# Four heads' decayed values on VectorE, w_in's conversion begun later, and decay tables made on the chip

## The chip, the cores and the metric

The kernel runs on one core of a Trainium2 chip. The metric is device time in microseconds (us), lower is better. A core has five instruction streams: TensorE (PE in the rows; PEld is its weight load), VectorE (DVE), ScalarE (ACT), GpSimd (POOL) and SyncE (SP), and 16 DMA engines that move data between device memory and the core's SBUF. Each stream is executed in its own order; what holds an instruction back is a semaphore that another stream or a DMA raises.

## The reference, cut to what matters

Three parts follow each other. The change touches only the first one and a preparation that runs beside it.

1. Decayed linear attention over 4 sequences of 768 tokens, 8 heads of 64: for each token, `state = gamma_h * state + k v^T` and `y = 0.125 * q state`, with `gamma_h = 1 - 2^(-5-h)`.
2. A capacity-limited mixture of experts: logits `x @ w_gate`, a greedy assignment of 3072 tokens to 8 experts of 384 places, and for each expert `relu(x w1) w2`.
3. A dense layer on the result: `softplus(x w_in) w_out`. All arithmetic has to keep fp32 quality, so the kernel splits weights and activations into a high and a low part of TensorE's reduced fp32 type and multiplies three times.

## The kernel before, in words

**Attention (class Attn).** The 24 chunks are 4 sequences of 6 chunks of 128 tokens. For one chunk TensorE computes: `qk` (L125, tile pA: k^T q of all heads, 16 products), which VectorE multiplies by the causal decay mask out of PSUM (L126, tile at); `y` (L142 within the chunk, and L138 from the state with decayed queries qs; tile pY), copied by ScalarE (L145, yT); `kv` (L155, tile pS: the state's update from decayed values vh), copied by ScalarE (L157, sb); and `xo` (L164, tile pX: yT times a matrix rx that transposes it and appends the 8 gate columns), copied by ScalarE (L168, xs) and stored by SP (L178). VectorE sums the four partial gate columns of pX (L173, `gate`) into L. The tiles pA, pX, pY and pS exist once each, so TensorE's `qk` of a chunk waits until `at` of the chunk before is read out, and its `xo` until both xs and the gate's sum of the chunk before are done.

Two decays come from the host. `qs` is q times a table (L106, GpSimd); the table has one 256 KB slice for each chunk of a sequence but the first, and SP loads that slice just before the chunk's q and k (L98). `vh` is v times one factor for each token and head (L108 to L115): eight ScalarE instructions of 128x64, one a head, for every chunk but a sequence's last.

The turn of the loop for chunk j (`emit`, L187) records in this order: load q,k of chunk j+3; store chunk j-2; `qk` of j+1; a side step; `xo` of j-1; `y` of j; a side step; the gate's sum of j-1; `kv` of j; load k,v of j+3; `qs` of j+2; `vh` of j+1; at every sixth chunk a block of 12 short VectorE instructions (`logits`, L383 to L399) that ranks the last six chunks' gate logits; a side step. There is no scheduler: each engine runs what was recorded for it in the order of the text. The DMAs of SP and ScalarE take eight completion semaphores in turn, so a DMA is also not issued before the one eight places ahead of it has landed.

**Conversion of w_in (class Conv), in the side steps.** w_in arrives as 64-bit numbers, 16 pieces of 512 KB (raw, five buffers, L230). A piece takes two ScalarE passes (L241, L243), one on GpSimd (L242), then VectorE (L256, L258), GpSimd (L259), ScalarE (L269, the high part wih) and VectorE (L264, the low part wil). `cv.ahead()` (L927) records the loads of the first four pieces before the loop; the steps begin with the turn of chunk 1 and are spread over the turns until the last.

After the attention (about 128 us) come the routing of the first expert's tokens, and then the eight experts with their dense layer (up to the end of the span), which the change does not touch.

Of the kernel before, what the change touches and what calls it, by code (L numbers as in the profile page):

```python
# [9 lines left out]
FT = mybir.dt.float32  # L10
# [5 lines left out]
AF = mybir.ActivationFunctionType  # L16
OP = mybir.AluOpType
# [3 lines left out]
def shape_tables(H, S):  # L21


    g = 1.0 - 2.0 ** (-5.0 - np.arange(H, dtype=np.float64))
    i = np.arange(128)
    t = i[:, None] + 128 * np.arange(S // 128)
    gk = g ** (-t[:, :, None].astype(np.float64))
    m = np.where(i[:, None] <= i, 0.125 * g[:, None, None] ** (i - i[:, None]).clip(0), 0.0)
    m = m.reshape(H // 2, 2, 128, 128).transpose(2, 1, 0, 3).reshape(128, -1)
    tab = np.concatenate([np.eye(128), m, gk.reshape(128, -1)], axis=1)  # L30
    gq = 0.125 * g[:, None] ** np.arange(S, dtype=np.float64)
    gq = np.repeat(gq.reshape(H // 2, 2, 1, S // 128, 128), 64, axis=2)
    gq = gq.transpose(1, 2, 3, 0, 4).reshape(128, -1)
    return tab.astype(np.float32), gq.astype(np.float32)


# [17 lines left out]
class Attn:  # L54
# [4 lines left out]
    def __init__(self, tc, ctx, ps, qk, kv, w_gate, tab, gqt, ident, L, xd, B, H, S):  # L59
        nc = self.nc = tc.nc  # L60
        self.ps = ps
        self.qk_in, self.kv_in, self.gq_in, self.L, self.xd, self.ident = qk, kv, gqt, L, xd, ident
        self.B, self.H, self.S = B, H, S
        self.NC = S // 128
        self.NCH = B * self.NC
        self.HP = HP = H // 2
        c = ctx.enter_context(tc.tile_pool(name="acst", bufs=1, side="right"))
        self.ld = ctx.enter_context(tc.tile_pool(name="ald", bufs=3, side="right"))
        self.wk = ctx.enter_context(tc.tile_pool(name="awk", bufs=2, side="right"))
        self.t = {}  # L70
        self.gq = c.tile([128, self.NC - 1, 512], FT, name="gqt")
        n = tab.shape[1] - 128
        ct = c.tile([128, n], FT, name="ctab")
        self.load(0, "qk")
        nc.scalar.dma_start(ct, tab[:, 128:])
        self.load(0, "kv")
        nc.scalar.dma_start(ident, tab[:, 0:128])
        self.cm = ct[:, 0:1024].rearrange("p (s a t) -> p s a t", s=2, a=HP)
        self.gk = ct[:, 1024:n].rearrange("p (c h) -> p c h", h=self.H)
        self.load(1)  # L80
        self.load(2)
        self.sb = []
        for i in range(2):
            self.sb.append(c.tile([128, HP, 64], FT, name=f"sb{i}"))
        self.rx = c.tile([128, HP, 136], FT, name="rx")
        nc.scalar.dma_start(self.rx[:, :, 128:136], w_gate.rearrange("(a p) e -> p a e", p=128))
        self.pS = self.ps.tile([128, HP, 128], FT, name="pS")
# [6 lines left out]
    def load(self, j, which=("qk", "kv")):  # L94
        for n in (which,) if isinstance(which, str) else which:
            t = self.t[n, j] = self.ld.tile([128, 2, 512], FT, name=n + "_t", bufs=4)
            if n == "qk" and 0 < j < self.NC:
                self.nc.sync.dma_start(self.gq[:, j - 1], self.gq_in[:, j * 512:(j + 1) * 512])  # L98
            self.nc.sync.dma_start(t, (self.qk_in if n == "qk" else self.kv_in)[j])

    def scale(self, j):

        c, nc = j % self.NC, self.nc
        if c:
            qs = self.t["qs", j] = self.wk.tile([128, self.HP, 128], FT, name="qs", bufs=2)
            nc.gpsimd.tensor_mul(qs.rearrange("p a t -> p (a t)"), self.t["qk", j][:, 0], self.gq[:, c - 1])  # L106

    def scale_v(self, j):  # L108

        c, nc = j % self.NC, self.nc  # L110
        if c < self.NC - 1:
            vh = self.t["vh", j] = self.wk.tile([128, self.H, 64], FT, name="vh", bufs=2)
            for h in range(self.H):
                nc.scalar.activation(vh[:, h], self.t["kv", j][:, 1, h * 64:h * 64 + 64], AF.Copy,
                                     scale=self.gk[:, c, h:h + 1])  # L115

    def qk(self, j):
        nc = self.nc
# [62 lines left out]
    def emit(self, side, logits):  # L181
        n = self.NCH
        self.qk(0)
        self.scale_v(0)
        self.scale(1)
        self.late_constants()
        for j in range(n):  # L187
            if j + 3 < n:
                self.load(j + 3, "qk")
            self.store(j - 2)  # L190
            if j + 1 < n:
                self.qk(j + 1)
            side(j, 0)
            if j:
                self.xo(j - 1)
            self.y(j)
            side(j, 1)
            if j:
                self.gate(j - 1)
            self.kv(j)  # L200
            if j + 3 < n:
                self.load(j + 3, "kv")
            if j + 2 < n:
                self.scale(j + 2)
            if j + 1 < n:
                self.scale_v(j + 1)
            if j:
                logits(j - 1)
            side(j, 2)
        self.store(n - 2)  # L210
        self.xo(n - 1)
        self.gate(n - 1)
        self.store(n - 1)
        logits(n - 1)
# [6 lines left out]
class Conv:  # L221
# [6 lines left out]
    def load(self, p):  # L228
        raw = self.raw[p] = self.st.tile([128, self.W, 2], I32, name="raw", bufs=self.bufs)
        self.nc.sync.dma_start(raw.rearrange("p n b -> p (n b)"), self.plan[p][0])  # L230

    def ahead(self, p=0):
        while self.loaded < min(p + self.bufs - 1, len(self.plan)):
            self.load(self.loaded)
            self.loaded += 1
# [659 lines left out]
def model(ctx, tc, qk, kv, w_gate, w1, w2, w_in, w_out, tab, gqt, out, B, H, S):  # L895
    nc = tc.nc
# [17 lines left out]
    cv = Conv(tc, c1, 512, cuts, 5, 2, (5, 4))  # L914
# [2 lines left out]
    a = Attn(tc, c2, aps, qk, kv, w_gate, tab, gqt, ident, L, xd, B, H, S)  # L917

    def side(j, part):
        if j:  # L920
            cv.step((3 * j - 2 + part) * 50 // 69)

    def logits(j):
        if j % 6 == 5:
            R.first_part(j - 5, j + 1)

    cv.ahead()  # L927
    a.emit(side, logits)
    cv.step(1000)
    c2.close()  # L930
# [41 lines left out]
```

## Time and profile before

| | |
|---|---|
| time, median of 3 runs | 1037.16 us (1035.96 to 1038.77) |
| the profiled execution | 1039.39 us, of which the span of the rows is 1037.6 us |
| TensorE busy | 994.5 us, 96% of the span |
| VectorE / ScalarE / GpSimd busy | 61% / 56% / 18% of the span |
| mean granted clock of TensorE | 0.987 |

Times in rows are microseconds from the span's start. A row of the timeline gives start, duration, engine, line, operation, output <- inputs, shapes, the count, and in brackets how long the engine had been idle before it and what ended that; instructions of one kind that follow each other are drawn together. In the rows by window a number after the window is its length, then busy time and instruction count of each engine, then the granted clock as a share of full speed, the mean busy share of the DMA engines and their GB/s.

### The profile page before, as it was taken

The numbers are of one execution on the slowest core, as the hardware profiler recorded it, in microseconds if no ns is written. First come the engines' busy times: TensorE is split into PE (matmuls) and PEld (weight loads), VectorE is DVE, ScalarE is ACT, GpSimd is POOL, SyncE is SP. The second block draws the span as 40 slices with busy tenths as digits, with TensorE's granted clock in tenths as the row PEclk, the third lists the DMA queues.
The fourth block names the chain that finished last, engine by engine and source line by source line (L and its number), as shares of the span: only waits on it lengthen the run. The fifth ranks groups of instructions, "written<-read, shape, count | busy, mean of one in ns | idle before, by whom it ended". The sixth has DMA issues, their size and how long they took to land.

```text
span 1037.6 us, 19094 instructions
## 1 busy us (share of the span) xinstructions
PE 994.5 (96%) x7266; PEld 901.9 (87%) x7266; DVE 636.3 (61%) x1649; ACT 585.0 (56%) x1245; POOL 186.1 (18%) x204
## 2 busy tenths in 40 slices
PE   5999878999999999999999999999999999999997
PEld 4888757978899889988998889888989899999996
DVE  3686687888766666766575567555665644454432
ACT  4897723676645563566446644665356546654664
POOL 4685422556210101010101010100010020001001
PEclk9998999999999999999999999999999999999999
DMA  9998434423141104110321023101410160014000
GB/s 358 401 405 306 146 96 137 128 82 112 54 142 32 31 21 124 50 31 11 117 67 32 11 92 92 31 1 52 122 32 1 52 192 1 1 41 123 1 1 31
DMA packets 41179, 97.55 MB, mean 94 GB/s; under 512 B 5376, under 2 KB 5504, under 8 KB 41088
## 3 DMA queue, kind: packets, MB, share of 16 engines
q1 hardware_dynamic: 36432, 83.12, 24.1%
q0 software_dynamic: 3840, 12.59, 3.7%
q8 instruction: 57, 0.93, 0.4%
q10 hardware_dynamic: 816, 0.63, 0.2%
q14 instruction: 34, 0.28, 0.1%
HBM read 83.73 MB, written 12.58 MB: 93 GB/s over the span
## 4 chain that ended last, share of the span: by engine, by line
PE 72%; issue 12%; POOL 5%; DVE 5%; DMA 2%; ACT 2%; another core or an unknown queue 0%; SPq 0%; ACTq 0%; POOLq 0%
PE h L659 11%; PE h L662 11%; PE h L660 10%; PE acc L757 7%; PE acc L762 7%; PE acc L758 7%; PE acc L651 3%; PE acc L653 3%; PE acc L652 3%; PE pX L164 2%; POOL wol L259 2%; PE pA L125 2%; POOL cA L242 2%; PE pY L142 2%; PE rt L406 2%
## 5 line engine op out<-in xcount | busy, mean ns | idle before, releaser
L723 DVE SCALAR_TENSOR_TENSOR gf<-h,sp 128x384 f32<-128x384 f32 x128 | 71.2, 556 | 185.2 <-ACT sp L721 185.0
L659 PE MATMUL h<-x2h,wih 128*128 128x384 f32 x512 | 176.5, 345 | 2.0 <-DVE xl L647 2.0
L660 PE MATMUL h<-x2h,wil 128*128 128x384 f32 x512 | 173.3, 338 | 0.0
L757 PE MATMUL acc<-whi,gh 128*128 128x512 f32 x384 | 153.2, 399 | 0.0
L758 PE MATMUL acc<-wlo,gh 128*128 128x512 f32 x384 | 151.2, 394 | 0.0
L719 ACT ACTIVATE sp<-h 128x384 f32<-128x384 f32 x128 | 62.6, 489 | 137.5 <-PE h L662 127.2
L643 ACT ACTIVATE h1h<-h 128x384 fp32r<-128x384 f32 x64 | 31.5, 492 | 148.8 <-PE h L662 105.5
L770 POOL DMA_INDIRECT out_dram<-rows,ix x24 | 25.3, 1053 | 501.4 <-ACT rows L768 498.0
L662 PE MATMUL h<-x2l,wih 128*128 128x384 f32 x512 | 112.8, 340 | 0.8 <-DVE x2l L647 0.6
L762 PE MATMUL acc<-whi,gl 128*128 128x512 f32 x384 | 111.2, 396 | 0.8 <-DVE gl L737 0.8
L659 PEld LDWEIGHTS h<-x2h,wih 128*128 128x128 f32 x512 | 96.6, 189 | 5.8 <-DVE xl L647 2.2
L660 PEld LDWEIGHTS h<-x2h,wil 128*128 128x128 f32 x512 | 96.6, 189 | 3.4
L662 PEld LDWEIGHTS h<-x2l,wih 128*128 128x128 f32 x512 | 92.1, 189 | 2.9 <-DVE x2l L647 2.9
L637 DVE TENSOR_TENSOR wlo<-wraw,whi 128x512 fp32r<-128x512 f32 x128 | 86.3, 689 | 6.1 <-ACT whi L636 6.1
L659 PE MATMUL h<-xh,whi 128*128 128x384 f32 x256 | 89.0, 348 | 0.7 <-ACT xh L646 0.7
L637 DVE TENSOR_TENSOR wlo<-wol,whi 128x512 fp32r<-128x512 f32 x128 | 89.0, 698 | 0.9 <-ACT whi L636 0.9
L651 PE MATMUL acc<-h1h,whi 128*128 128x384 f32 x256 | 88.4, 345 | 0.0
L762 PEld LDWEIGHTS acc<-whi,gl 128*128 128x128 f32 x384 | 72.0, 188 | 18.6 <-DVE gl L737 1.4
L660 PE MATMUL h<-xh,wlo 128*128 128x384 f32 x256 | 86.8, 339 | 0.0
L636 ACT ACTIVATE whi<-wraw 128x512 fp32r<-128x512 f32 x128 | 76.6, 624 | 17.1 <-DMA wraw<-in_moe_w_dram 14.2
L653 PE MATMUL acc<-h1l,whi 128*128 128x384 f32 x256 | 86.1, 336 | 0.0
L652 PE MATMUL acc<-h1h,wlo 128*128 128x384 f32 x256 | 86.1, 336 | 0.0
(201 smaller groups left out, 1932.1 us busy)
## 6 DMA issues: line engine op xcount, KB each, us to landing
wraw<-in_moe_w_dram SPq DMA_DIRECT2D x128, 256.0 KB, 2.7
qk_t<-in_qk_dram SPq DMA_DIRECT2D x24, 512.0 KB, 8.8
kv_t<-in_kv_dram SPq DMA_DIRECT2D x24, 512.0 KB, 6.4
raw<-in_moe_w_in_dram SPq DMA_DIRECT2D x16, 512.0 KB, 7.0
raw<-in_moe_w_out_dram SPq DMA_DIRECT2D x32, 256.0 KB, 2.8
xd<-xs SPq DMA_DIRECT2D x24, 256.0 KB, 4.7
gqt<-in_gqt_dram SPq DMA_DIRECT2D x5, 256.0 KB
ctab<-in_tab_dram ACTq DMA_DIRECT2D x1, 536.0 KB
```

What stands on the lines that cost most here:

```text
L636: nc.scalar.activation(hi, raw, AF.Copy)
L637: nc.vector.tensor_tensor(lo, raw, hi.bitcast(FT), op=OP.subtract)
L651: nc.tensor.matmul(ps, wh, ah, start=start, stop=False)
L652: nc.tensor.matmul(ps, wl, ah, start=False, stop=False)
L653: nc.tensor.matmul(ps, wh, al, start=False, stop=stop)
L659: mm(ps, wh(d), ah[:, d], start=d == 0, stop=False)
L660: mm(ps, wl(d), ah[:, d], start=False, stop=False)
L662: mm(ps, wh(d), al[:, d], start=False, stop=d == 3)
L723: nc.vector.scalar_tensor_tensor(g, ps, 0.0, a, op0=OP.max, op1=OP.add)
L757: nc.tensor.matmul(ps, gh[:, s], wh, start=f == 0, stop=False)
L758: nc.tensor.matmul(ps, gh[:, s], wl, start=False, stop=False)
L762: nc.tensor.matmul(ps, gl[:, s], wh, start=False, stop=f == 15)
```

## The change

Four edits, all in the attention.

- `vh`: ScalarE keeps heads 0 to 3 (four instructions of 128x64); heads 4 to 7 become one VectorE product of 128x256 (v times the factors, broadcast over 64 columns), recorded behind them.
- The decay table of q: the host sends one chunk's table and the 20 step factors (`gqb`, 128x532, one DMA on ScalarE's queue, 272 KB); in the first sequence `scale(j)` makes each chunk's slice by four VectorE instructions of 128x128. SP's five slice loads are gone.
- w_in: no load is recorded before the loop. `begin` records one load in each side step from chunk 2 on until four are out; the conversion steps start at chunk 4 and are spread over the turns 4 to 23.
- The gate's sum of chunk j-1 is recorded behind `vh` and the turn's last side step, just before `logits`.

```diff
--- before.py
+++ after.py
@@ -28,9 +28,11 @@
     m = np.where(i[:, None] <= i, 0.125 * g[:, None, None] ** (i - i[:, None]).clip(0), 0.0)
     m = m.reshape(H // 2, 2, 128, 128).transpose(2, 1, 0, 3).reshape(128, -1)
     tab = np.concatenate([np.eye(128), m, gk.reshape(128, -1)], axis=1)
-    gq = 0.125 * g[:, None] ** np.arange(S, dtype=np.float64)
-    gq = np.repeat(gq.reshape(H // 2, 2, 1, S // 128, 128), 64, axis=2)
-    gq = gq.transpose(1, 2, 3, 0, 4).reshape(128, -1)
+    gq = np.repeat((0.125 * g[:, None] ** i).reshape(H // 2, 2, 1, 128), 64, axis=2)
+    gq = gq.transpose(1, 2, 0, 3).reshape(128, -1)
+    gs = g[:, None] ** (128.0 * np.arange(1, S // 128))
+    gs = np.repeat(gs.reshape(H // 2, 2, 1, -1), 64, axis=2).transpose(1, 2, 3, 0).reshape(128, -1)
+    gq = np.concatenate([gs, gq], axis=1)
     return tab.astype(np.float32), gq.astype(np.float32)
 
 
@@ -71,8 +73,10 @@
         self.gq = c.tile([128, self.NC - 1, 512], FT, name="gqt")
         n = tab.shape[1] - 128
         ct = c.tile([128, n], FT, name="ctab")
+        self.gb = c.tile([128, gqt.shape[1]], FT, name="gqb")
         self.load(0, "qk")
         nc.scalar.dma_start(ct, tab[:, 128:])
+        nc.scalar.dma_start(self.gb, gqt)
         self.load(0, "kv")
         nc.scalar.dma_start(ident, tab[:, 0:128])
         self.cm = ct[:, 0:1024].rearrange("p (s a t) -> p s a t", s=2, a=HP)
@@ -94,13 +98,17 @@
     def load(self, j, which=("qk", "kv")):
         for n in (which,) if isinstance(which, str) else which:
             t = self.t[n, j] = self.ld.tile([128, 2, 512], FT, name=n + "_t", bufs=4)
-            if n == "qk" and 0 < j < self.NC:
-                self.nc.sync.dma_start(self.gq[:, j - 1], self.gq_in[:, j * 512:(j + 1) * 512])
             self.nc.sync.dma_start(t, (self.qk_in if n == "qk" else self.kv_in)[j])
 
     def scale(self, j):
 
         c, nc = j % self.NC, self.nc
+        if c and j == c:
+            n = (self.NC - 1) * self.HP
+            for hp in range(self.HP):
+                s = slice(hp * 128, hp * 128 + 128)
+                nc.vector.tensor_scalar(self.gq[:, c - 1, s], self.gb[:, n:][:, s],
+                                        self.gb[:, (c - 1) * self.HP + hp:(c - 1) * self.HP + hp + 1], None, op0=OP.mult)
         if c:
             qs = self.t["qs", j] = self.wk.tile([128, self.HP, 128], FT, name="qs", bufs=2)
             nc.gpsimd.tensor_mul(qs.rearrange("p a t -> p (a t)"), self.t["qk", j][:, 0], self.gq[:, c - 1])
@@ -110,9 +118,10 @@
         c, nc = j % self.NC, self.nc
         if c < self.NC - 1:
             vh = self.t["vh", j] = self.wk.tile([128, self.H, 64], FT, name="vh", bufs=2)
-            for h in range(self.H):
-                nc.scalar.activation(vh[:, h], self.t["kv", j][:, 1, h * 64:h * 64 + 64], AF.Copy,
-                                     scale=self.gk[:, c, h:h + 1])
+            v, n = self.t["kv", j][:, 1].rearrange("p (h d) -> p h d", d=64), self.H // 2
+            for h in range(n):
+                nc.scalar.activation(vh[:, h], v[:, h], AF.Copy, scale=self.gk[:, c, h:h + 1])
+            nc.vector.tensor_tensor(vh[:, n:], v[:, n:], self.gk[:, c, n:, None].to_broadcast([128, n, 64]), op=OP.mult)
 
     def qk(self, j):
         nc = self.nc
@@ -195,8 +204,6 @@
                 self.xo(j - 1)
             self.y(j)
             side(j, 1)
-            if j:
-                self.gate(j - 1)
             self.kv(j)
             if j + 3 < n:
                 self.load(j + 3, "kv")
@@ -204,9 +211,10 @@
                 self.scale(j + 2)
             if j + 1 < n:
                 self.scale_v(j + 1)
+            side(j, 2)
             if j:
+                self.gate(j - 1)
                 logits(j - 1)
-            side(j, 2)
         self.store(n - 2)
         self.xo(n - 1)
         self.gate(n - 1)
@@ -228,6 +236,11 @@
     def load(self, p):
         raw = self.raw[p] = self.st.tile([128, self.W, 2], I32, name="raw", bufs=self.bufs)
         self.nc.sync.dma_start(raw.rearrange("p n b -> p (n b)"), self.plan[p][0])
+
+    def begin(self):
+        if self.loaded < min(self.bufs - 1, len(self.plan)):
+            self.load(self.loaded)
+            self.loaded += 1
 
     def ahead(self, p=0):
         while self.loaded < min(p + self.bufs - 1, len(self.plan)):
@@ -917,14 +930,16 @@
     a = Attn(tc, c2, aps, qk, kv, w_gate, tab, gqt, ident, L, xd, B, H, S)
 
     def side(j, part):
-        if j:
-            cv.step((3 * j - 2 + part) * 50 // 69)
+        n = 3 * j + part
+        if n >= 6:
+            cv.begin()
+        if n >= 12:
+            cv.step((n - 11) * 50 // 60)
 
     def logits(j):
         if j % 6 == 5:
             R.first_part(j - 5, j + 1)
 
-    cv.ahead()
     a.emit(side, logits)
     cv.step(1000)
     c2.close()
```

SP's stream, at the loads of chunks 1 to 3 of the first sequence (qk_t is q and k of a chunk, kv_t its k and v, raw a piece of w_in, gqt a slice of the decay table). Before:

```order
L99 DMA kv_t_161<-in_kv_dram 128x1024
L98 DMA gqt_150<-in_gqt_dram 128x512 [waits DMAHW0_49]
L99 DMA qk_t_163<-in_qk_dram 128x1024 [waits DMAHW1_49]
L99 DMA kv_t_166<-in_kv_dram 128x1024 [waits DMAHW2_49]
L230 DMA raw_173<-in_moe2_w_in_dram 128x1024 [waits DMAHW3_49]
L230 DMA raw_175<-in_moe2_w_in_dram 128x1024 [waits DMAHW4_49]
L230 DMA raw_177<-in_moe2_w_in_dram 128x1024 [waits DMAHW5_49]
L230 DMA raw_179<-in_moe2_w_in_dram 128x1024 [waits DMAHW6_49]
L98 DMA gqt_150<-in_gqt_dram 128x512 [waits DMAHW7_49]
L99 DMA qk_t_207<-in_qk_dram 128x1024 [waits DMAHW0_49]
```

The same place now, from the load of k and v of chunk 1 on:

```order
L101 DMA kv_t_162<-in_kv_dram 128x1024
L101 DMA qk_t_164<-in_qk_dram 128x1024 [waits DMAHW0_49]
L101 DMA kv_t_166<-in_kv_dram 128x1024 [waits DMAHW1_49]
L101 DMA qk_t_200<-in_qk_dram 128x1024 [waits DMAHW2_49]
L101 DMA kv_t_233<-in_kv_dram 128x1024 [waits DMAHW3_49]
L101 DMA qk_t_247<-in_qk_dram 128x1024 [waits DMAHW4_49,PE_49]
L101 DMA kv_t_295<-in_kv_dram 128x1024 [waits DVE_49,DMAHW5_49,PE_49,Activation_49]
L101 DMA qk_t_310<-in_qk_dram 128x1024 [waits DMAHW6_49,Pool_49]
L187 DMA xd_63<-xs_265 128x512 [waits DMAHW7_49,Activation_49]
L238 DMA raw_324<-in_moe2_w_in_dram 128x1024 [waits DMAHW0_49]
```

The q and k of chunk 3 (qk_t_207 before, qk_t_200 now) stood behind four pieces of w_in and two table slices; now it stands where the first piece stood, and waits only for the semaphore that k and v of chunk 0 raise (DMAHW2).

VectorE's stream, in the turn of chunk 7, right behind the first `logits` block (whose last row is the first one shown). Before:

```order
L258 TENSOR_SCALAR cA_496<-cA_496 128x512
L126 TENSOR_TENSOR at_687<-pA_688,ctab_151 128x1024
L264 TENSOR_TENSOR wil_67<-cA_407,wih_66 128x4x128
L173 TENSOR_REDUCE L_64<-pX_698 128x8
L256 SCALAR_TENSOR_TENSOR cB_587<-raw_379,cB_587 128x512
L126 TENSOR_TENSOR at_755<-pA_756,ctab_151 128x1024
```

And now:

```order
L412 TENSOR_TENSOR G_140<-kx_139,thr0_85 128x276
L135 TENSOR_TENSOR at_659<-pA_660,ctab_151 128x1024
L277 TENSOR_TENSOR wil_67<-cA_491,wih_66 128x4x128
L269 SCALAR_TENSOR_TENSOR cB_565<-raw_394,cB_565 128x512
L124 TENSOR_TENSOR vh_714<-kv_t_569,ctab_151 128x256
L271 TENSOR_SCALAR cA_564<-cA_564 128x512
L182 TENSOR_REDUCE L_64<-pX_671 128x8
L135 TENSOR_TENSOR at_731<-pA_732,ctab_151 128x1024
```

The gate's sum (L173, now L182) has moved from the second place behind `at` to the fifth, just ahead of the next `at`, and the product of four heads' values (L124) and one more conversion step stand in front of it.

## Rows read from the trace of the kernel before

**Rows 1.** Three stretches of the attention by window (window, length, busy times, clock, DMA).

```profile
0.00:22.60 22.60, 10.97 (x136) 9.85 (x137) 7.39 (x29) 10.56 (x30) 7.34 (x20) 0.97 0.95 350
22.60:29.40 6.80, 6.77 (x72) 5.93 (x72) 2.35 (x4) 3.09 (x9) 5.58 (x6) 0.60 1.04 408
29.40:76.00 46.60, 45.71 (x732) 40.26 (x728) 34.05 (x63) 43.78 (x128) 33.57 (x24) 1.00 1.03 404
```

**Rows 2.** The chain that ended last, in the first 30 us (start, length, what).

```profile
1.69 10.43 DMA rx<-in_moe_w_gate_dram
...
13.46 9.04 DMA qk_t<-in_qk_dram
```

**Rows 3.** TensorE's timeline, chunks 2 to 4 and one undisturbed turn.

```profile
18.50 0.64 PE L155 MATMUL pS<-vh,kv_t 128*64 128x64 f32 x16
22.63 2.08 PE L125 MATMUL pA<-qk_t 64*128 64x128 f32 x16 [3.50 <-DMA qk_t<-in_qk_dram]
...
29.41 1.16 PE L125 MATMUL pA<-qk_t 64*128 64x128 f32 x16
...
55.64 1.16 PE L125 MATMUL pA<-qk_t 64*128 64x128 f32 x16
...
59.94 1.16 PE L125 MATMUL pA<-qk_t 64*128 64x128 f32 x16
```

**Rows 4.** SyncE's timeline: the first pieces of w_in.

```profile
8.39 4.55 SPq L230 DMA_DIRECT2D raw<-in_moe_w_in_dram  x4
```

**Rows 5.** DMA issues (KB each, median us to landing), from the page.

```profile
qk_t<-in_qk_dram SPq DMA_DIRECT2D x24, 512.0 KB, 8.8
...
raw<-in_moe_w_in_dram SPq DMA_DIRECT2D x16, 512.0 KB, 7.0
...
gqt<-in_gqt_dram SPq DMA_DIRECT2D x5, 256.0 KB
```

**Rows 6.** TensorE's timeline where it waited for the mask product `at`.

```profile
51.33 1.16 PE L125 MATMUL pA<-qk_t 64*128 64x128 f32 x16 [0.68 <-DVE at L126]
...
79.75 2.08 PE L125 MATMUL pA<-qk_t 64*128 64x128 f32 x16 [3.59 <-DVE at L126]
...
86.97 1.16 PE L125 MATMUL pA<-qk_t 64*128 64x128 f32 x16
...
109.60 1.16 PE L125 MATMUL pA<-qk_t 64*128 64x128 f32 x16 [1.53 <-DVE at L126]
```

**Rows 7.** The logits block on VectorE: held up by GpSimd, and alone (128.75 on).

```profile
75.09 2.50 POOL L106 TENSOR_TENSOR qs<-qk_t,gqt 128x512 f32<-128x512 f32 x2
75.18 1.20 DVE L394 SCALAR_TENSOR_TENSOR kf<-sg,unas 128x6 f32<-128x6 int32 x1
...
128.75 0.20 DVE L383 TENSOR_REDUCE m<-L 128x6 f32<-128x48 f32 x1
...
130.51 0.30 DVE L399 TENSOR_TENSOR G<-kx,thr 128x276 bf16<-128x276 f16 x1
```

**Rows 8.** The same VectorE product beside two kinds of GpSimd work.

```profile
55.01 1.27 POOL L259 TENSOR_TENSOR cA<-cA,cB 128x512 int32<-128x512 int32 x1 [0.36 <-DVE cA L258]
55.07 1.76 DVE L264 TENSOR_TENSOR wil<-cA,wih 128x512 fp32r<-128x512 f32 x1
...
82.03 1.49 POOL L242 TENSOR_SCALAR cA<-cA 128x512 f32<-128x512 f32 x1
83.02 0.68 DVE L264 TENSOR_TENSOR wil<-cA,wih 128x512 fp32r<-128x512 f32 x1
```

**Rows 9.** One chunk's decayed values on ScalarE, and a gate's sum that waited.

```profile
15.19 2.00 ACT L114 ACTIVATE vh<-kv_t,ctab 128x64 f32<-128x64 f32 x8
...
104.29 0.19 DVE L173 TENSOR_REDUCE L<-pX 128x8 f32<-128x32 f32 x1 [1.51 <-ACT xs L168]
```

**Rows 10.** VectorE's mask product by form, 29.4 to 76 us (count, busy, mean ns).

```profile
L126 DVE TENSOR_TENSOR at<-pA,ctab 128x1024 f32<-128x1024 f32 x10 | 12.2, 1221 | 6.4 <-PE pA L125 6.3
```

**Rows 11.** VectorE's timeline: the shift step of the conversion.

```profile
36.06 0.42 DVE L258 TENSOR_SCALAR cA<-cA 128x512 int32<-128x512 int32 x1
```

## The prediction

> **What bounds the kernel now.** I read the windows first, then the chain of waits, then TensorE's timeline. The change only touches the attention, the first 128 us; what follows is handed the same data and starts when the attention ends, so what it saves or costs there is taken one for one. In the windows [rows 1] the reader is to see two things. From 29.4 to 76 us TensorE is busy 45.71 of 46.60 us at the full clock, with the DMA engines full as well (share 1.03, 404 GB/s) and ScalarE nearly so (43.78 us). Ahead of that, in the first 22.6 us, TensorE is busy for less than half of the time while the DMA engines are already at 0.95, and in the next 6.8 us its granted clock is 0.60.
>
> The chain of waits says why [rows 2]: a small transfer (the gate's columns into rx) lands at 12.1 us and releases SP, which only then gets to issue q and k of chunk 3, at 13.46; those land 9.04 us later. In between SP had been issuing four pieces of w_in [rows 4]. TensorE's timeline shows the price [rows 3]: it ended chunk 1's state update at 18.50 + 0.64 = 19.14, stood idle for 3.50 us, and began chunk 3's products at 22.63 at the lower of its two clock levels (1.2 GHz: 16 products take 2.08 us, against 1.16 us at 2.4 GHz). The turn that begins there took 29.41 - 22.63 = 6.78 us; an undisturbed one takes 59.94 - 55.64 = 4.30.
>
> Later the bound is TensorE itself, but for three places where its next products waited for `at` on VectorE: 0.68, 3.59 and 1.53 us [rows 6], each right after a logits block. After the second one the clock was again at the lower level, and the turn took 86.97 - 79.75 = 7.22 us, 2.92 more than 4.30. The three cost 0.68 + 3.59 + 2.92 + 1.53 = 8.7 us.
>
> **The change part by part.**
>
> *Loads.* The four pieces of w_in (2.1 MB) and two table slices no longer stand ahead of chunk 3's q and k, which are now issued where the first piece was, at about 8.4 us [rows 4]. At 9.04 us to landing [rows 2], near the median of 8.8 [rows 5], they are there at 17.4 us, before TensorE asks at 19.14. The wait of 3.50 us goes, and with no idle stretch I expect the clock to stay up, so the 6.78 us turn becomes 4.30: 2.48 more. What is late next there is TensorE's own chain. Together -6.0 us. Bounds: if the landing slipped as much as 2 us more, about 1.7 + 0.3 us of it would be absorbed first, so 0 to -6.5.
>
> The five slices (1.28 MB) are replaced by one transfer of 0.27 MB on ScalarE's queue; it moves beside k and v of chunk 0 and q of chunk 1 as the first slice did. In the first turns I take 0, between -0.5 and +0.5 by its share at 0.35 MB a us [rows 1].
>
> *The same loads later.* The pieces return from chunk 2 on, four in two turns, and then 12 in the turns of chunks 4 to 17. A turn then moves 1.05 MB of q, k and v, 0.26 MB of stores and about 0.45 MB of w_in, 1.76 MB, or 4.36 us at 404 GB/s: the DMA engines, full at a turn of 4.30 before, want slightly more than a turn. I count what must have arrived when chunk 12 starts: 26 transfers of 0.52 MB, about 10 pieces, 8 stores and 0.9 MB of tables, 21.8 MB, so about 56 us from a start at 2 us. TensorE is ready for it at 23.4 + 8 x 4.2 = 57 us. That is 1 us of lead, where a transfer shares the engines with some that were issued after it. I charge +1.0 us; bounds 0 (the stops at the logits give lead) and +2.7: before, the 7.2 MB issued up to chunk 3's q and k would have been there at 2 + 7.2 / 0.404 = 19.8 us, and landed at 22.5 [rows 2], so a transfer wants up to 2.7 us of lead, and chunk 12 could lack it all.
>
> *Decayed values.* ScalarE gives up four of eight instructions, half of 2.00 us [rows 9], in 20 of 24 chunks. From 29.4 to 76 us it was busy 43.78 / 46.60 x 4.30 = 4.04 us a turn; it falls to about 3.5, with the denser conversion counted. That by itself does not move TensorE, but ScalarE's late xs had held the gate's sum, and behind it a logits block, by 1.51 us [rows 9]; that wait goes.
>
> The new VectorE product has 256 elements a partition from two SBUF inputs. No such row exists. Below it stands 0.30 us for 276 elements of 16 bits [rows 7], above it 0.68 us for 512 fp32 elements, alone, and 1.76 us when GpSimd is in the way [rows 8]. I take 0.4, near the shorter row. VectorE was busy 34.05 / 46.60 x 4.30 = 3.14 us a turn [rows 1]; with 0.33 for the product (five chunks of six) and 0.2 for the denser conversion it is at 3.7 of 4.30, with waits for GpSimd in it as they were. So it stays beside TensorE in an ordinary turn, with 0.6 us to spare: if that is gone, each turn costs the difference.
>
> *What stands against it.* A product that starts beside GpSimd's two-input addition took 1.76 us instead of 0.68: it ended 0.55 us after that addition; beside GpSimd's one-input maximum the same form took 0.68 [rows 8]. In the trace it is the two-input work of GpSimd (qs and L259, about 1.27 us each, some 2.1 of 4.3 us a turn) that holds VectorE up. The Trainium skill's "SBUF — State Buffer", section "Who interferes with whom", has it broader: a VectorE instruction with two SBUF inputs contends with any GpSimd instruction that reads SBUF, and the later of the two is blocked for the whole of the other. The first pair of rows agrees, the second does not; by the rule the new product would meet such work for 33.57 of 46.60 us [rows 1], and the last rival below would be the likelier for it. I go by the rows.
>
> *Gate's sum.* It is 0.19 us either way [rows 9]. Moved, it no longer makes VectorE wait for xs, but two conversion steps and the new product now stand ahead of it, and TensorE's next `xo` needs it, since pX exists once. In an ordinary turn VectorE starts `at` 1.2 us into the turn and has 1.22 [rows 10] + 1.5 + 0.4 + 0.2 of work, so the sum is done at about 4.5, before 5.4, when `xo` asks. Behind a logits block it is not: `at` is already late, and `xo` then waits about 1 us for the sum.
>
> *Logits.* A block takes 130.51 + 0.30 - 128.75 = 2.06 us alone; held up by GpSimd single instructions of it take 1.20 [rows 7], beside a pair of decayed queries of 2.50. I charge 2.06 + 1.3 of being held up, of which the slack behind `at` absorbs most, plus the late sum: 2.5 us each, 7.5 for three, against 8.7: -1.2. Bounds: 1 us each (-5.7) and, with a fall of the clock behind two of them, 4.8 each (+5.7).
>
> *Tables.* 20 instructions of 128x128, between nothing and the 0.42 us of an instruction of four times the columns [rows 11]; at 0.2 each 0.8 a turn, in turns in which VectorE has no conversion to do and was busy 7.39 of 22.6 us before. Hidden: 0; without the cover +0.8 in a turn.
>
> Sum: -6.0 + 0 + 1.0 - 1.2 + 0.4 for small waits of ScalarE for GpSimd, now that it runs at the head of its queue, = -5.8. Against the profiled execution, 1039.4 us (its span of 1037.6 and 1.8 around it), that is 1033.6; this execution is 2.2 us above the median of the runs, 1037.2, so the forecast is **1031.4 us**.
>
> **The rivals.**
>
> *More than that.* ScalarE's relief keeps the logits blocks on time, and none of them stops TensorE for long or drops its clock: the terms are -6.0 and 3 x 1 against 8.7, -11.7, so 1025.5. For it: the blocks alone are 2 us, and two of the three cost under 1.6 us before. Against it: 0.4 us more VectorE work in front of each.
>
> *The transfers take it back.* If the DMA engines bound the middle, only the 1.0 MB of table slices that is no longer moved is gained, 1.0 / 0.404 = 2.5 us: 1034.7. For it: share 1.03 [rows 1]. Against it: before, they were full as well and TensorE did not wait.
>
> *The early wait does not go.* Chunk 3's q and k land as late as before for another reason, and the rest is a wash: 1037.
>
> *VectorE becomes the bound, and it is slower.* Decayed queries on GpSimd are released when TensorE has read the former ones, about when VectorE comes to the new product; if the two meet in each turn, the product takes 0.4 + 1.25 (half of the pair in [rows 7]), the turn needs 3.7 + 1.25 = 4.95, and 16 turns lose 0.65 each, +10.4. With -6.0 that is 1041.6. It decides from 0.6 us of being held up per turn. Against it: GpSimd's two-input work fills 2.1 of 4.3 us, so a meeting by chance holds the product for half of 1.27 us in half of the turns, 0.3 us, within the 0.6 to spare.
>
> **How the numbers follow.** Forecast 0.50, own range 1028 to 1034.5; more than that 0.17; transfers 0.15; wait stays 0.06; VectorE 0.12. A measurement of this kernel can tell about 0.3%, 3.1 us, from no change: faster is below 1034.1, slower above 1040.3. Faster: 0.46 of the forecast, 0.17, and 0.07 of the transfers, 0.70. Slower: 0.10 of the VectorE case and 0.01 of the wait. Within: 0.19. The range that leaves out a tenth on each side runs from 1025 to 1039.
>
> **What would show it.** In the profile after, chunk 3's 16 products begin near 19.2 us with no idle time before them and take 1.16 us, and chunk 4's begin near 23.5. The DMA rows before 17 us hold no piece of w_in. VectorE's new product takes about 0.4 us, and more only beside GpSimd's two-input work. TensorE's waits are for `at` and for the gate's sum behind three logits blocks, under 3 us each. I am wrong if TensorE waits for q and k in the middle, if it waits for VectorE in ordinary turns, or if its clock falls where it did not.

## The result: slower by 0.94%, and the profile after

The changed kernel takes 1047.17 us (median of 6 runs, 1044.66 to 1049.96), the kernel before 1036.96 us beside it; the ratio is 1.0094, 95% interval 1.0079 to 1.0110. The forecast of 1031.4 us was wrong in sign, and the time lies above the range. The profiled execution took 1048.33 us (span 1046.6).

TensorE's timeline after, to be laid beside [rows 3, 6] (start, length, engine, line, what, and in brackets idle time ahead and its releaser):

```profile
19.23 1.16 PE L134 MATMUL pA<-qk_t 64*128 64x128 f32 x16
...
23.53 1.16 PE L134 MATMUL pA<-qk_t 64*128 64x128 f32 x16
...
35.70 2.15 PE L173 MATMUL pX<-rx,yT 128*128 128x136 f32 x8 [2.40 <-DVE L L182]
...
39.87 1.16 PE L134 MATMUL pA<-qk_t 64*128 64x128 f32 x16
...
43.57 1.16 PE L134 MATMUL pA<-qk_t 64*128 64x128 f32 x16
45.97 1.17 PE L173 MATMUL pX<-rx,yT 128*128 128x136 f32 x8 [1.24 <-DVE L L182]
...
51.53 1.18 PE L134 MATMUL pA<-qk_t 64*128 64x128 f32 x16 [2.31 <-DVE at L135]
53.59 2.15 PE L173 MATMUL pX<-rx,yT 128*128 128x136 f32 x8 [0.88 <-DVE L L182]
...
59.46 1.16 PE L134 MATMUL pA<-qk_t 64*128 64x128 f32 x16
...
84.54 1.16 PE L134 MATMUL pA<-qk_t 64*128 64x128 f32 x16 [2.31 <-DVE at L135]
...
116.42 1.22 PE L134 MATMUL pA<-qk_t 64*128 64x128 f32 x16 [2.31 <-DVE at L135]
```

Chunk 3 now begins at 19.23 with no idle time, and chunk 4 at 23.53 where it was 29.41 [rows 3]. Then the lead is lost. At 35.70 the product `xo` (into pX) of chunk 4 waits 2.40 us for the gate's sum, and its eight products take 2.15 us, against 1.17 for the same eight at 45.97: the lower clock level again. At each of the three logits blocks TensorE waits 2.31 us for `at`, and 0.84 to 0.90 us more for the sum behind it.

The waits of TensorE, grouped, 0 to 140 us (total us, times, longest):

```profile
PE pX L173 <- DVE L L182: 9.9, 10, 2.4
PE pA L134 <- DMA qk_t<-in_qk_dram: 8.1, 2, 6.5
PE pA L134 <- DVE at L135: 6.9, 3, 2.3
```

The first row is new; before, no `xo` waited for the sum. The q and k that it waits for are those of chunks 0 and 1 only, so none in the middle.

The windows after, to be laid beside [rows 1]:

```profile
0.00:22.60 22.60, 14.55 (x186) 13.03 (x188) 11.39 (x48) 7.28 (x19) 6.05 (x19) 1.00 0.91 335
22.60:29.40 6.80, 6.80 (x118) 6.12 (x115) 3.08 (x10) 4.22 (x13) 2.54 (x2) 1.00 1.01 363
29.40:76.00 46.60, 38.56 (x545) 33.59 (x545) 35.21 (x57) 30.49 (x71) 31.13 (x22) 0.89 0.91 343
```

In the first two TensorE does 304 operations where it did 208, at a granted clock of 1.00 (before: 0.97 and 0.60). In the third it is busy 38.56 us of 46.60 where it was 45.71, ScalarE falls from 43.78 to 30.49, the DMA share from 1.03 to 0.91: none of these three is the bound any more. VectorE is not full either (35.21). What rules is the order of its instructions, and what each has to wait for.

A balance by stages says where the 10 us are. It goes by the starts of the qk products in the timelines, in us. "Blocks" are the six turns from chunk 8 to 10, 14 to 16 and 20 to 22, in which a logits block is felt; "ordinary" are the eight from chunk 10 to 14 and 16 to 20. The four stages add up to the start of chunk 22. The experiments below are in the same table.

| kernel | to chunk 4 | 4 to 8 | blocks | ordinary | chunk 22 |
|---|---|---|---|---|---|
| before | 29.41 | 16.87 | 35.34 | 32.28 | 113.90 |
| after | 23.53 | 20.04 | 45.89 | 34.88 | 124.34 |
| e1 sum early | 23.11 | 18.06 | 44.11 | 32.30 | 117.58 |
| e2 values on ScalarE | 23.53 | 20.54 | 37.23 | 34.23 | 115.53 |
| e3 both | 23.07 | 18.74 | 37.18 | 33.21 | 112.20 |
| e4 before, sum late | 29.59 | 16.87 | 35.33 | 32.29 | 114.08 |
| e5 after, blocks spread | 22.62 | 18.83 | 31.90 | 38.38 | 111.73 |
| e6 after, no product on GpSimd | 22.89 | 18.83 | 28.20 | 34.88 | 104.80 |
| e7 e3, spread | 23.46 | 18.75 | 29.21 | 33.70 | 105.12 |
| e8 e1, spread | 24.21 | 18.06 | 33.86 | 34.32 | 110.45 |
| e9 before, spread | 30.07 | 16.85 | 26.49 | 32.78 | 106.19 |
| e10 e7, conversion from chunk 2 | 22.71 | 19.69 | 27.18 | 33.66 | 103.24 |
| e11 e7, conversion from chunk 3 | 23.39 | 19.56 | 28.43 | 34.56 | 105.94 |
| e12 e10, values on VectorE | 24.03 | 21.11 | 28.11 | 35.36 | 108.61 |
| e13 e10, in steps | 23.44 | 16.14 | 29.16 | 34.52 | 103.26 |
| e14 e13, sum ahead | 23.31 | 17.03 | 27.94 | 34.76 | 103.04 |

After against before: -5.9 to chunk 4, +3.2 where the conversion starts, +10.6 at the blocks, +2.6 in ordinary turns, +1.0 behind chunk 22, so +11.5 at the last `xo` (138.16 against 126.67). The span grows by 9.0, so 2.5 us come back behind the attention. That is within what executions differ by there: from the last `xo` to the end the sixteen traces take 907.2 to 912.5 us (910.9 before, 908.4 after). A row is one execution, and some lie far from their kernel's median (e2 and e3 at 1038.69 and 1034.82 us against 1042.72 and 1038.32, e8 at 1037.97 against 1034.52), so verdicts below go by the medians. Where a run is given in us, that is its ratio less one, times 1037.

VectorE and GpSimd around the first block after, between TensorE's qk products of chunks 7 (39.87) and 9 (51.53):

```profile
42.74 2.70 POOL L114 TENSOR_TENSOR qs<-qk_t,gqt 128x512 f32<-128x512 f32 x2
42.82 1.50 DVE L124 TENSOR_TENSOR vh<-kv_t,ctab 128x256 f32<-128x256 f32 x1
44.24 1.49 DVE L271 TENSOR_SCALAR cA<-cA 128x512 int32<-128x512 int32 x1
45.65 0.18 DVE L182 TENSOR_REDUCE L<-pX 128x8 f32<-128x32 f32 x1
45.80 1.28 POOL L272 TENSOR_TENSOR cA<-cA,cB 128x512 int32<-128x512 int32 x1 [0.36 <-DVE cA L271]
45.86 0.20 DVE L396 TENSOR_REDUCE m<-L 128x6 f32<-128x48 f32 x1
46.10 1.05 DVE L397 TENSOR_TENSOR lm<-L,m 128x48 f32<-128x48 f32 x1
...
48.50 1.27 POOL L114 TENSOR_TENSOR qs<-qk_t,gqt 128x512 f32<-128x512 f32 x1
48.59 1.20 DVE L407 SCALAR_TENSOR_TENSOR kf<-sg,unas 128x6 f32<-128x6 int32 x1
...
50.04 0.30 DVE L412 TENSOR_TENSOR G<-kx,thr 128x276 bf16<-128x276 f16 x1
50.26 1.22 DVE L135 TENSOR_TENSOR at<-pA,ctab 128x1024 f32<-128x1024 f32 x1
```

Two of GpSimd's products run from 42.74 to 45.44. The first VectorE instruction beside them, the new product, takes 1.50 us, the second, a shift that took 0.42 [rows 11], takes 1.49: one for each of GpSimd's pair. Only then comes the sum, and behind it the block, from 45.86 to 50.34, 4.5 us against 2.06 alone [rows 7]; in it `lm` lasts until the addition beside it ends, and `kf`, 6 elements wide, as long as the next product of GpSimd. Then `at`, for which TensorE waits. The block as such is not what is new: before, the three took 3.09, 5.50 and 3.29 us (46.72 to 49.81, 72.45 to 77.95, 104.52 to 107.81), held up by GpSimd as well, after 4.48 to 4.49 each, 0.5 us more on average. New are the 3 us of product and shift ahead of it, with the sum in between, in all three turns.

The same in an ordinary turn, around the qk products of chunk 11 (63.76), `xo` of TensorE with it:

```profile
62.31 1.66 POOL L272 TENSOR_TENSOR cA<-cA,cB 128x512 int32<-128x512 int32 x1 [4.06 <-DVE cA L271]
62.75 1.50 DVE L124 TENSOR_TENSOR vh<-kv_t,ctab 128x256 f32<-128x256 f32 x1
63.93 1.66 POOL L255 TENSOR_SCALAR cA<-cA 128x512 f32<-128x512 f32 x1
64.17 1.09 DVE L269 SCALAR_TENSOR_TENSOR cB<-raw,cB 128x512 int32<-128x512 int32 x1
65.18 0.18 DVE L182 TENSOR_REDUCE L<-pX 128x8 f32<-128x32 f32 x1
65.51 1.17 PE L173 MATMUL pX<-rx,yT 128*128 128x136 f32 x8 [0.58 <-DVE L L182]
```

Here it is the conversion's addition that holds the product up (it ends 0.28 us after it), the next step is lengthened from 0.68 to 1.09, and the sum behind them makes `xo` 0.58 us late.

### The profile page after: what moved, and what is told of

The parts are those of the page before. It is cut to its first block, busy times and chain, and to the rows that moved or that the text cites. A ratio compares the mean times of both kernels' runs of the same rounds, so it can differ in the third digit from the quotient of the medians.

```text
span 1046.6 us, 19079 instructions
## 1 busy us (share of the span) xinstructions
PE 994.8 (95%) x7266; PEld 901.8 (86%) x7266; DVE 657.5 (63%) x1689; ACT 568.5 (54%) x1165; POOL 188.3 (18%) x204
## 4 chain that ended last, share of the span: by engine, by line
PE 69%; issue 14%; DVE 8%; POOL 5%; DMA 2%; ACT 1%; SPq 0%; POOLq 0%; ACTq 0%; DVEq 0%
PE h L672 10%; PE h L675 10%; PE h L673 10%; PE acc L770 7%; PE acc L771 7%; PE acc L775 7%; PE acc L664 3%; PE acc L666 3%; PE acc L665 3%; POOL wol L272 2%; POOL cA L255 2%; PE rt L419 2%; PE pX L173 2%; PE pY L151 1%; PE pA L134 1%
```

## The experiments

**Which part costs: each undone (e1 to e3), and the late sum alone on the kernel before (e4).**

```diff
 e1: self.y(j); side(j, 1)
+    if j: self.gate(j - 1)              # as before the change
     ... logits(j - 1)                   # without the gate ahead of it
 e2: for h in range(2 * n):              # all eight heads on ScalarE
-    nc.vector.tensor_tensor(vh[:, n:], v[:, n:], ...)
 e3: e1 and e2 together: the loads, the conversion's start and the tables are left
 e4: before.py with side(j, 2) and gate(j - 1) placed as after the change
```

> The changed kernel with one edit undone: the gate's sum stands ahead of the chunk's state update again. Theory G (the late sum holds TensorE at pX, and the idle time lets its clock fall): the 9.9 us of waits for the sum go, and with them most of the turns at the lower clock, so 1031 to 1035 us. Theory V (the product of four heads' values on VectorE is the load that does not fit): little changes, 1043 to 1047 us. Theory C (the conversion, denser and begun at chunk 4, is what does not fit): 1043 to 1047 us.

> The changed kernel with the other edit undone: all eight heads' values on ScalarE again, the gate's sum late as in the change. Theory G: the sum is still last in VectorE's turn, 1041 to 1047 us. Theory V: VectorE has 0.89 us less in five of six turns and keeps up, 1031 to 1035 us. Theory C: 1043 to 1047 us.

> Gate's sum and values both undone: what is left of the change is the later loads and conversion of w_in and the decay tables made on the chip. Theories G and V: the 6 us won at chunk 3 stay, and the logits blocks cost as before, 1029 to 1034 us. Theory C: the waits for VectorE stay although its other load is gone, 1040 us or more.

> The kernel before with one edit alone: the gate's sum behind the values and the turn's last side step. Theory G: the sum waits behind conversion steps and TensorE behind the sum, 1042 to 1050 us. Theories V and C: VectorE has time to spare without the product and with the conversion as it was, 1036 to 1039 us.

Measured: e1 1039.73 us, ratio 1.0016 [1.0000, 1.0033]; e2 1042.72, 1.0055 [1.0036, 1.0074]; e3 1038.32, 1.0012 [0.9998, 1.0026]; e4 1038.80, 1.0019 [1.0004, 1.0034]. The late sum costs 2.0 us on the kernel before, 4.5 with the loads (e2 less e3) and 8.1 with loads and product (after less e1). The product costs 0.4 us with an early sum (e1 less e3) and 4.0 with a late one (after less e2). Each of these is uncertain by about 2 us. So by these ratios the two cost 3.6 us more together than one by one, uncertain by 3.3: just clear of the noise. That the product is cheap with an early sum is less sure: in the traced executions e1 is 5.4 us behind e3 at the last `xo` (130.12 against 124.74), and e8 below finds 5.4 by the medians. The stages agree on the place: the product is paid at the blocks (37 to 44 or 46 us), the late sum in ordinary turns and at the conversion's start; on the kernel before, e4's stages show nothing of its 2.0 us. And the loads alone, with 6 us gained by chunk 4, end by the median where the kernel before ended; in the traced execution 1.7 us of lead are left at chunk 22. In e3 the first block gives most of it back, of which the second returns a part (11.29 us for its two turns against 15.19 before):

```profile
50.33 1.16 PE L133 MATMUL pA<-qk_t 64*128 64x128 f32 x16 [4.14 <-DVE at L134]
```

4.14 us where the kernel before lost 0.68 [rows 6]. The block lasts 5.79 us there (43.35 to 49.14) in place of 3.09: three of its instructions take over 1 us beside GpSimd's, where one did before. Where the block falls within GpSimd's work has changed; why it fell so was not tried.

In e1 the sum does not stand behind the product, but the block does. VectorE, GpSimd and TensorE there:

```profile
42.46 2.51 POOL L114 TENSOR_TENSOR qs<-qk_t,gqt 128x512 f32<-128x512 f32 x2
42.50 1.30 DVE L400 TENSOR_TENSOR lm<-lm,desc 128x48 f32<-128x48 f32 x1
43.72 1.28 DVE L401 TENSOR_SCALAR sg<-m 128x6 int32<-128x6 int32 x1
...
44.92 1.28 POOL L273 TENSOR_TENSOR cA<-cA,cB 128x512 int32<-128x512 int32 x1
45.04 1.19 DVE L405 TENSOR_TENSOR ik<-m,sg 128x6 int32<-128x6 int32 x1
...
48.77 2.08 PE L134 MATMUL pA<-qk_t 64*128 64x128 f32 x16 [2.82 <-DVE at L135]
```

Three tiny instructions, 0.15 to 0.20 us each alone, take 3.77 us beside three of GpSimd's, and TensorE's wait ends at the lower clock.

**Is it GpSimd that holds VectorE up (e6)?** The decayed queries are replaced by the decay table itself; VectorE's instructions are those of after.

```diff
-            nc.gpsimd.tensor_mul(qs..., self.t["qk", j][:, 0], self.gq[:, c - 1])
+            self.t["qs", j] = self.gq[:, c - 1]...
```

> The changed kernel without GpSimd's product for the decayed queries: the state is multiplied by the decay table itself, so this part of the computation is left out; VectorE's and TensorE's instructions are the same. Theory K (VectorE's instructions are long because they are held up by GpSimd's two-input work): the values' product falls from 0.89 to about 0.6 us, the logits blocks from 4.5 to under 3.5 us, 1035 to 1041 us. Theory B or S alone (VectorE has too much work of its own, whoever is beside it): 1044 to 1047 us.

Measured: 1029.05, ratio 0.9924 [0.9896, 0.9951], some 18 us under the changed kernel. VectorE's groups by form, 29.4 to 127 us (count, busy, mean ns), first of after and then of e6, where the window also holds the block behind the attention:

```profile
L124 DVE TENSOR_TENSOR vh<-kv_t,ctab 128x256 f32<-128x256 f32 x14 | 12.5, 890 | 0.0
L271 DVE TENSOR_SCALAR cA<-cA 128x512 int32<-128x512 int32 x15 | 10.9, 725 | 0.3 <-POOL cA L255 0.3
L407 DVE SCALAR_TENSOR_TENSOR kf<-sg,unas 128x6 f32<-128x6 int32 x3 | 3.6, 1200 | 0.1
```

```profile
L123 DVE TENSOR_TENSOR vh<-kv_t,ctab 128x256 f32<-128x256 f32 x15 | 10.7, 714 | 0.0
L270 DVE TENSOR_SCALAR cA<-cA 128x512 int32<-128x512 int32 x16 | 7.5, 468 | 0.3 <-POOL cA L254 0.3
L406 DVE SCALAR_TENSOR_TENSOR kf<-sg,unas 128x6 f32<-128x6 int32 x4 | 0.7, 166 | 0.1
```

`kf` falls from 1200 ns to 166, the shift from 725 to 468. Around the first block product and shift take 0.41 us each again, and the block 3.2. The six turns with a block fall from 45.89 to 28.20 us; the ordinary turns stay at 34.88, since what holds the product up there is the conversion's addition, which e6 keeps (1.50 us at 54.90, beside the addition of 54.47). So the meetings with GpSimd's product account for what the blocks cost, not for all of the loss. The kernel before had such meetings too [rows 7] and was not run without that product, so the 18 us need not all be of the change's making. (Its absence also frees GpSimd and a wait of TensorE; that no wait for `qs` stands among TensorE's in after speaks against this being the gain.)

**Is it the lump (e5, e7, e8, e9)?** The block's instructions are spread over four turns, at most three in each; e5 does it to after, e7 to e3, e8 to e1, e9 to the kernel before.

```diff
     def logits(j):
         if j % 6 == 5:
-            R.first_part(j - 5, j + 1)
+            ranks.append(R.first_part(j - 5, j + 1))
+        while ranks:
+            if next(ranks[0], ranks) is ranks:
+                ranks.pop(0)
+            if j + 1 < NCH:
+                break
```

> The changed kernel, with the 12 instructions of a logits block recorded three a turn over four turns. Theory B (VectorE fits an ordinary turn and loses at the block, which comes as one lump): the three waits of 2.31 us and the turns at the lower clock behind them go, 1034 to 1039 us. Theory S (the late sum loses in ordinary turns as well, the block is only where it shows): 1042 to 1047 us.

> Only the later loads and the tables made on the chip (gate's sum early, all values on ScalarE), with the logits block spread over four turns. Theory B: the 6 us won at chunk 3 are kept at last, and most of the 8.7 us that the blocks cost before are won too, 1024 to 1030 us. A rival (the transfers or the denser conversion take the 6 us back): 1034 to 1038 us.

> The changed kernel with the gate's sum early and the logits block spread over four turns: beside it the loads-only kernel with the same spread took 1029 us, and differs only in the four heads' values on ScalarE. If VectorE has room for the values' product once sum and block are out of its way: 1028 to 1030 us. If the product is too much for an ordinary turn (it took 0.89 us in the changed kernel beside GpSimd): 1032 to 1037 us.

> The kernel before with the logits block spread over four turns, nothing else. Theory B: the waits for the mask product and the turn at the lower clock, 8.7 us in the profile, go for the most part, 1029 to 1033 us. The rival: VectorE's turns are full anyway and the block's work only moves, 1035 to 1038 us.

Measured: e5 1040.09, ratio 1.0025 [1.0009, 1.0041]; e7 1028.99, 0.9922 [0.9894, 0.9949]; e8 1034.52, 0.9974 [0.9957, 0.9991]; e9 1029.02, 0.9916 [0.9891, 0.9941]. Spreading gains 7 to 9 us on three kernels and 4.4 on e1, and e9 beats both kernels. Its first block, on VectorE:

```profile
47.34 0.20 DVE L383 TENSOR_REDUCE m<-L 128x6 f32<-128x48 f32 x1
47.58 1.26 DVE L384 TENSOR_TENSOR lm<-L,m 128x48 f32<-128x48 f32 x1
48.88 0.17 DVE L385 TENSOR_SCALAR m<-m 128x6 f32<-128x6 f32 x1
48.96 0.42 DVE L258 TENSOR_SCALAR cA<-cA 128x512 int32<-128x512 int32 x1
49.29 1.22 DVE L126 TENSOR_TENSOR at<-pA,ctab 128x1024 f32<-128x1024 f32 x1
```

One instruction is held up as ever (1.26), but only three stand ahead of `at`, and TensorE goes from chunk to chunk in 4.30 and 4.43 us there. With the blocks out of the way the product's own price shows: e8 less e7, 5.4 us, uncertain by 3.4. In e5 `xo` waits 10.1 us for VectorE, for the sum or for the block's instructions that now stand ahead of it, and its ordinary turns are the longest of all, 38.38.

**Where do the 6 us of the loads go (e10 to e14)?** e7 starts as early as predicted, and is no faster than e9. Of the 5.5 us by which its lead over e9 shrinks from chunk 4 to 22, 1.9 lie before chunk 8, where the conversion starts, 2.7 at the spread blocks and 0.9 in ordinary turns. e10 and e11 start it elsewhere; e13 starts it in steps; e12 and e14 add the values' product to e10, and the gate ahead of the side step to e13.

```diff
 e10: if n >= 1: cv.begin()     if n >= 6: cv.step((n - 5) * 50 // 66)
 e11: if n >= 5: cv.begin()     if n >= 9: cv.step((n - 8) * 50 // 63)
 e13: if n in (5, 7): cv.step(1 if n == 5 else 2)      # size() of one piece each
      if n >= 9: cv.step(2 + (n - 8) * 48 // 63)
```

> The loads-only kernel with spread logits (1029 us), but w_in's loads from chunk 0's second side step on, behind the load of chunk 3's q and k, and its conversion from chunk 2 on over 22 turns instead of from chunk 4 over 20. Theory C (the conversion, begun later and packed denser, gives back on VectorE and ScalarE the 6.6 us won at chunk 3): 1022 to 1026 us. Theory D (the DMA engines are full and take it back whenever the pieces are loaded): 1028 to 1031 us.

> The same with the loads from chunk 1's last side step on and the conversion from chunk 3, over 21 turns. Theory C: between the two, 1025 to 1028 us. Theory D: 1028 to 1031 us.

> The kernel with the conversion from chunk 2, with four heads' values on VectorE as in the change. If the product fits beside the less dense conversion: within 1 us of that kernel. If VectorE is the tighter engine of the two: 2 to 6 us slower than it.

> The kernel with loads from chunk 0, conversion from chunk 2 and spread logits (1029.4 us), whose conversion now starts in steps: ScalarE's passes of the first piece in the last side step of chunk 1, of the second in chunk 2, VectorE's first step in chunk 3. Theory P (the conversion's first steps come as one lump of four ScalarE passes, on which VectorE waits with the gate's sum behind it; that lump costs TensorE 3 to 4 us wherever it stands, and before it stood under the wait for chunk 3): the waits of 1.23 and 2.06 us behind the start go, 1025 to 1028 us. The rival (TensorE's 6 us are lost to full DMA engines or to dense turns, and the waits would only move): 1028.5 to 1031 us.

> The same with the gate's sum recorded ahead of the turn's second side step too, so that nothing of the conversion's middle step stands between TensorE's xo and the sum. If the sum still holds TensorE up now and then: 1 to 2 us faster than that kernel. If VectorE's wait for xs in front of it costs more than it saves: as fast or up to 2 us slower.

Measured: e10 1029.43, ratio 0.9926 [0.9900, 0.9952]; e11 1030.11, 0.9929 [0.9904, 0.9953]; e12 1034.70, 0.9976 [0.9956, 0.9996]; e13 1028.95, 0.9918 [0.9898, 0.9939]; e14 1031.08, 0.9946 [0.9925, 0.9967]. e10, e11 and e13 lie where it was expected that full DMA engines or dense turns take the 6 us back. The rows speak against the DMA engines: in e7, e10 and e13 none of the four computing engines waits for q, k, v or a piece of w_in from 15 us to the end of the attention. The start costs the same wherever it is put (19.69 and 19.56 us from chunk 4 to 8). In e10, VectorE and TensorE:

```profile
24.16 0.69 DVE L269 SCALAR_TENSOR_TENSOR cB<-raw,cB 128x512 int32<-128x512 int32 x1 [3.32 <-ACT cB L256]
...
25.10 1.17 PE L172 MATMUL pX<-rx,yT 128*128 128x136 f32 x8 [1.23 <-DVE L L181]
...
31.50 1.19 PE L172 MATMUL pX<-rx,yT 128*128 128x136 f32 x8 [2.06 <-ACT yT L153]
```

The first step waits 3.32 us for pieces that ScalarE and GpSimd prepare in turn, with the gate's sum queued behind it. The kernel before paid the same, on VectorE:

```profile
20.45 0.69 DVE L256 SCALAR_TENSOR_TENSOR cB<-raw,cB 128x512 int32<-128x512 int32 x1 [3.25 <-ACT cB L243]
```

But there it lay inside TensorE's wait for chunk 3, which ended at 22.63 [rows 3], and nobody missed the time. e13 takes the price away (16.14 us from chunk 4 to 8, the least of all), is 7.3 us ahead of e9 at chunk 8, and is back to 2.9 at chunk 22 and 1.3 at the last `xo` (117.45 against 118.73); its time is that of e9. Three waits of TensorE, 4.6 us together, take much of the 6.1 us that are lost:

```profile
56.10 1.17 PE L172 MATMUL pX<-rx,yT 128*128 128x136 f32 x8 [1.31 <-DVE L L181]
...
74.24 1.17 PE L172 MATMUL pX<-rx,yT 128*128 128x136 f32 x8 [1.66 <-DVE L L181]
...
113.91 1.17 PE L172 MATMUL pX<-rx,yT 128*128 128x136 f32 x8 [1.61 <-DVE L L181]
```

Right ahead of the sum, in the first two, stands a conversion step that took 1.76 and 1.75 us in place of 0.68, each beside GpSimd's product for the decayed queries. Putting the gate ahead (e14) mends these two waits, but makes VectorE wait for `xs` up to 2.31 us, and the last `xo` starts at 117.38, as in e13. By the ratios e14 is 2.9 us slower, uncertain by 3.1; its trace shows nothing of that in the attention, so the cause stays open. e12 repeats the price of the product, 5.2 us over e10.

## Why the prediction was wrong, point by point

*The loads: right.* -6.0 was forecast at chunk 4, -5.9 came, with the clock up and the idle time gone.

*The tables and the later transfers: right in kind.* Chunks 1 and 2 begin within 0.15 us of before. The +1.0 for a late chunk 12 did not show: TensorE waits for no q and k behind chunk 1. The rival "the transfers take it back" and the rival "the early wait does not go" fall with the same rows. No row was behind the 0.4 us for ScalarE's waits.

*The decayed values: the price alone right, the step wrong.* Alone the product takes 0.41 to 0.42 us, as forecast. In its turns it takes 890 ns on average. "So it stays beside TensorE in an ordinary turn, with 0.6 us to spare" is one of the steps that failed. I had drawn the meetings at random, half of 1.27 us in half of the turns, 0.3 us. The average hold-up of the product is not far from that, 0.48; but it is not spread evenly. Of the fourteen behind 29.4 us six took 0.41 to 0.42 us, three 0.82 and five 1.49 to 1.50, at the same places of each sequence, and a long one right ahead of each of the three blocks. And others in the turn were held up with it: the shift took 725 ns on average, in the kernel before 488.

*The gate's sum: half right.* I named what stands in front of it and that pX exists once, and forecast about 1 us of wait behind a block: 0.84 to 0.90 came. That an ordinary turn would have it by 4.5 us failed with the step above: in the turn that began at 59.46 it was done after 5.9 us. And I missed the start of the conversion, where the sum is queued behind an instruction that itself waits 3.32 us, for TensorE's wait at 35.70:

```profile
33.58 0.69 DVE L269 SCALAR_TENSOR_TENSOR cB<-raw,cB 128x512 int32<-128x512 int32 x1 [3.32 <-ACT cB L256]
```

*The logits: the mis-sized term, and the main error.* "2.5 us each, 7.5 for three, against 8.7" became 20.1 (the blocks' 45.89 us less six turns of 4.30), against 9.5 by the same count before. A block was 4.5 us long and not 2.06 + 1.3; the three of the kernel before already took 4.0 on average. Ahead of it stood the product and a held-up shift, and the sum came behind. Of the 20.1 us, 12.6 are TensorE's waits, for `at` and at the `xo` ahead of and behind it (two of these, 0.91 us each, are put down to ScalarE, but end 0.1 us behind the sum); about 7.1 are products at the lower clock, which now came behind all three blocks, where before it was one. Even my bound of 4.8 each was too low, because I priced block, product and sum each against the slack of a turn, which exists once. The runs point that way: 2.0 for the late sum, 0.4 for the product and 1.2 for the loads, each taken by itself, and together 9.7, which is 6.1 more than their sum, uncertain by about 3.5.

*The right rival.* "VectorE becomes the bound, and it is slower" had 0.12 and 1041.6 us. Its mechanism, GpSimd's two-input work holding the product up, is in the rows, and e6 shows it where the decayed queries meet product, shift and block. Its size and place were not right: it had 0.65 us lost in each of 16 turns, where the eight ordinary ones lost 0.33 each (+2.6) and the blocks more (+10.6). That its time came nearest is in part luck. The Trainium skill's rule ("SBUF — State Buffer", "Who interferes with whom"), set aside for the rows, pointed at this outcome. The runs do not go as far on one side: beside GpSimd's one-input maximum a step of VectorE was lengthened (1.09 at 64.17) but ended 0.33 us before it, so it was not blocked for the whole. And what I counted, work with two inputs, was too little: VectorE's instructions with one tensor input (the shift, 1.49 us; `sg`, 1.28) were held up beside GpSimd's two-input work too.

*What stays open.* Why all of the lead of 7.3 us in e13 shrinks: its three waits for the sum add to 4.6 us with their cause on VectorE, and the rows name a meeting with GpSimd for two of them, but no run tried these apart. Nor is it known why the product seems cheap with the block in one lump (0.4 us) and dear with it spread (5.4 and 5.2); by their uncertainties these could be nearer to each other.

## What to carry to other kernels

Slack in a turn is spent once: add up what an engine does in a turn with its measured hold-ups, all edits together, before calling any of them hidden. Put the small instruction that frees a single buffer ahead of filler work, and never behind one that waits for another engine. Break a lump of side work into a few instructions a turn (8.7 us here) before shortening the wait in front of it, and ask what else was hidden in an idle stretch that is to go.

## What was not expected of the hardware

A VectorE instruction of 6 elements a partition took as long as the GpSimd product of 512 beside it (1.20 beside 1.27 us, 166 ns on average without that product). A pair of GpSimd's products held up two VectorE instructions in a row (1.50 and 1.49 us). And the clock fell behind a shorter wait than I had seen before: the products behind 2.40 us took 2.15 us in place of 1.17, where those behind the 1.53 us of [rows 6] ran at the full clock. The length of the wait alone does not tell: the same eight took 1.17 us behind 2.41 us in e5 and e6, and behind 2.06 us 1.19 in e10 but 2.18 in e12.
